# Up to 64 leftover tokens of the first expert moved behind the shared tile; the third expert's loads moved behind the gathers

## The chip, the cores and the metric

One core of one Trainium2 chip runs the program. The metric is device time in microseconds; lower is better. The kernel before took 619.59 us, the median of three runs (619.25 to 619.83).

## The reference

Three layers follow each other on 2304 tokens of 512 numbers: block-causal attention, a dense layer with the maximum of three products, and a routed layer with eight experts. The change is in the last one:

```python
do_compute = x @ w_skip > 0
xc = x[do_compute]
logits = xc @ w_gate
e_idx = np.argmax(logits, axis=1)
gate_w = softmax(logits)[chosen expert]
for e in range(E):
    h = np.maximum(xc[e_idx == e] @ w1[e], 0.0)      # 512 -> 1024
    y[e_idx == e] = gate_w * (h @ w2[e])             # 1024 -> 512
out = x.copy(); out[do_compute] = xc + y
```

For the inputs that are drawn, 532 tokens are computed. By the reference the experts get, sorted by size, 153, 117, 116, 69, 60 and 17 tokens, and two experts get none.

## The kernel before

Attention and the dense layer fill the first 527 us. They write x to DRAM (`x2`) and a table of token numbers by expert. `count` (line 890) ranks the experts by their tokens, writes the ranks to `order` and three numbers to `counts`: `first` (tokens of the largest expert), `kind` and `over`. Class `Moe2` does the routed layer.

An expert has four weight pieces of 1 MB (1,048,576 bytes): `w1` by columns (pieces 0 and 1) and `w2` by rows (2 and 3). Piece i of the expert of rank s is numbered q = 4s + i. A piece is loaded by SP into one of six raw buffers (`raw_of`, line 1055: `raw0` to `raw2`, the first four rows of `xa`, `raw4`, the first four of `xb`) or, for q 22 and 23, into `raw22` and `xgw`. ACT copies the piece to fp32r (`split_hi`, "hi") and DVE writes the rest (`split_lo`, "lo"), in two halves each. The next piece for the same buffer can be loaded only then.

The tokens of an expert are gathered from `x2` by indirect DMAs of POOL, 128 rows of 2 KB each (`gather`). `block(s)` works off the first 128 tokens of the expert of rank s: TensorE does each product in three fp32r passes (hi by hi, lo by hi, hi by lo), 12 matmuls of 512 columns for each half of `w1` and 24 for `w2`. It turns the activations between them (`turn`, four 128x128 transposes) and turns the tokens of the next block. `finish` multiplies by the gate, adds x and scatters the rows to `out`. While block s runs, it splits the pieces q = 4s + 2 to 4s + 5 and orders the loads of q = 4s + 8 to 4s + 11, each behind the splits that free its buffer.

The order of the work is written out by hand in `run`: the gathers, `block(0)`, the gather of the shared tile, `extra`, blocks 1 to 3, `joint`. `extra` works off the tokens 129 to 256 of the largest expert (gathered into `xg2`) by the same 48 matmuls, if `first > P`; `turn_extra` (line 1257, within block 0) turns them. `joint` works off the experts of ranks 4 and 5 in one tile where the second has at most 64 tokens: 64 tokens of each, in native fp32, straight from the raw buffers. `pairs` issues for every contraction slice d two matmuls, one for each expert, that take 64 columns of the array each; TensorE runs a native fp32 matmul as two instructions. So the program waits in `joint` for the raw pieces themselves: q 16 (`raw0`) and q 20 (`raw4`) first.

SP takes its instructions in order: the table loads (`load_table`), the stores of the last x, the loads of q 8 to 11, 22 and 23 (`load_late`), and then those of the blocks. So does POOL: the gathers, then the scatter of each block, and the gather of the shared tile behind the scatter of block 0.

Of the kernel before, what the change touches and what calls it, by code (L numbers as in the profile page):

```python
# [395 lines left out]
@with_exitstack  # L396
def kernel(
    ctx: ExitStack,
    tc: tile.TileContext,
    kqT: bass.AP,  # L400
    kq0: bass.AP,
    v: bass.AP,
    w1: bass.AP,
    w2: bass.AP,
    w3: bass.AP,
    w_out: bass.AP,
    w_route: bass.AP,
    m2_w1: bass.AP,
    m2_w2: bass.AP,
    cst: bass.AP,  # L410
    aux: bass.AP,
    out: bass.AP,
):
# [24 lines left out]
    row0 = const.tile([P, 1], F32, name="row0")  # L438
    two = const.tile([P, 2], F32, name="two")
    wr_sb = const.tile([P, ND, NG], F32, name="wr_sb")  # L440

    _moe1_phase(tc, nc, const, small, locals())


def _moe1_phase(tc, nc, const, small, g):
# [12 lines left out]
    with ExitStack() as st_y:  # L458
# [431 lines left out]
        def count():  # L890
# [7 lines left out]
            first, kind, over = (by[:, n:n + 1] for n in range(3))  # L898
# [3 lines left out]
            nc.vector.tensor_copy(first, by[:, 3:4])  # L902
# [5 lines left out]
            nc.vector.tensor_tensor(two[:, 0:1], used[:, 1:2], used[:, 2:3], op=ALU.is_gt)  # L908
            nc.vector.tensor_copy(counts, by[0:1])
# [17 lines left out]
        def constants():  # L927
# [4 lines left out]
            nc.gpsimd.memset(ones, 1.0)  # L932
            nc.gpsimd.iota(tid, pattern=[[P, NT // P]], base=0, channel_multiplier=1,
# [95 lines left out]
class Moe2:  # L1029
    def __init__(self, tc, nc, small, ypool, tmp, wpool, xp, ps_m, g):  # L1030
# [3 lines left out]
        self.order, self.pick, self.two = g["order"], g["pick"], g["two"]  # L1034
# [6 lines left out]
        self.xg4 = self.right.tile([P, DM], F32, name="xg4")  # L1041
        self.lo = []
# [21 lines left out]
    def load(self, e, i, raw):  # L1064
# [5 lines left out]
        self.nc.sync.dma_start(out=raw, in_=src.rearrange("o (c p) n -> p (o c) n", p=P))  # L1070

    def load_q(self, q, raw=None):
        self.load(self.eid[q // 4], q % 4, self.raw_of(q) if raw is None else raw)
# [40 lines left out]
    def load_table(self):  # L1114
        small, sync, table = self.small, self.nc.sync, self.table
        self.te = small.tile([P, NE, 2], F32, tag="te", name="te", bufs=1)
        self.te1 = small.tile([P, 2], F32, tag="te1", name="te1", bufs=1)
        self.te5 = small.tile([P, NE, 2], F32, tag="te5", name="te5", bufs=1)
        tv = table.rearrange("(e n) t -> n e t", e=NE)
        sync.dma_start(out=self.te, in_=tv[0:P])  # L1120
        sync.dma_start(out=self.te1, in_=table[bass.ds(self.eid[0] * CAP + P, P), :])
        sync.dma_start(out=self.te5[64:P], in_=tv[0:64])

    def load_late(self):
        self.get_order(range(2, 6))
        self.load_raws(12)
        self.raw22 = self.ypool.tile([P, 4, 512], F32, tag="h_h", name="raw22")
        for i in (2, 3):
            self.load_q(20 + i, self.joint_w(1, i))
# [73 lines left out]
    def block(self, s, load=True, nxt=True, plain=False):  # L1203
# [52 lines left out]
        if s == 0:  # L1256
            self.turn_extra()
# [83 lines left out]
    def index_tables(self):  # L1341
# [11 lines left out]
        nc.vector.tensor_copy(tt[:, NE, :], self.te1)  # L1353
# [4 lines left out]
    def index_joint(self):  # L1358
# [11 lines left out]
        nc.vector.tensor_copy(ti[r, 4:5], tt[r, 4, 0:1])  # L1370

    def run(self):
# [3 lines left out]
        first, kind, over = self.regs  # L1376
# [15 lines left out]
        with tc.If(kind > 2, preferred_fallthrough_block=False) as branch:  # L1392
# [99 lines left out]
```

## Time and profile before

| | |
|---|---|
| median of three runs | 619.59 us (619.25 to 619.83) |
| the profiled execution | 618.85 us |
| its span, first to last instruction | 616.9 us |
| PE busy | 595.0 us (96%) |
| DVE, ACT, POOL busy | 57%, 51%, 7% |
| mean granted TensorE clock | 0.997 |
| moved by DMA | 68.65 MB, mean 111 GB/s |

The span is what the instruction records cover; 1.95 us of the execution's time lie around it. A busy PE is not PE at its peak, since matmuls are pipelined; PEld is the loading of weights, which runs beside them, and the start of a weight load shows best when TensorE goes on. The granted clock 1.0 is 2.4 GHz and 0.5 is 1.2 GHz. In the timeline, a bracket tells how long the engine was idle before and what released it.

### The profile page before, as it was taken

The numbers are of one execution on the slowest core, as the hardware profiler recorded it, in microseconds if no ns is written. First come the engines' busy times: TensorE is split into PE (matmuls) and PEld (weight loads), VectorE is DVE, ScalarE is ACT, GpSimd is POOL, SyncE is SP. The second block draws the span as 40 slices with busy tenths as digits, with TensorE's granted clock in tenths as the row PEclk, the third lists the DMA queues.
The fourth block names the chain that finished last, engine by engine and source line by source line (L and its number), as shares of the span: only waits on it lengthen the run. The fifth ranks groups of instructions, "written<-read, shape, count | busy, mean of one in ns | idle before, by whom it ended". The sixth has DMA issues, their size and how long they took to land. (4 is left out here: it accounts for less than half of the span.)

```text
span 616.9 us, 11455 instructions
## 1 busy us (share of the span) xinstructions
PE 595.0 (96%) x4164; PEld 494.2 (80%) x4164; DVE 350.2 (57%) x1001; ACT 316.2 (51%) x816; POOL 44.1 (7%) x99
## 2 busy tenths in 40 slices
PE   6889999999999999999999999999999999999995
PEld 3568797779888888987888887988888997778851
DVE  4899999833645426655165563465642675317920
ACT  4998769933656424545145444446541541236820
POOL 1000000002000010000100001000002002311100
PEclk9999999999999999999999999999999999999998
DMA  6565654321101120102211222200005841695960
GB/s 184 154 202 161 190 158 153 118 90 55 54 28 41 54 88 24 40 24 68 92 44 51 60 75 89 61 22 23 1 25 189 301 153 50 195 380 191 313 231 19
DMA packets 58887, 68.65 MB, mean 111 GB/s; under 512 B 7380, under 2 KB 40404, under 8 KB 58816
## 3 DMA queue, kind: packets, MB, share of 16 engines
q1 hardware_dynamic: 57152, 64.68, 33.0%
q0 software_dynamic: 1664, 3.09, 1.5%
q8 instruction: 37, 0.61, 0.4%
q14 instruction: 34, 0.28, 0.2%
HBM read 57.06 MB, written 11.18 MB: 111 GB/s over the span
## 5 line engine op out<-in xcount | busy, mean ns | idle before, releaser
L730 PE MATMUL ps_h<-x,w 128*128 128x384 f32 x1296 | 243.3, 341 | 0.0
L730 PEld LDWEIGHTS ps_h<-x,w 128*128 128x128 f32 x1296 | 222.8, 188 | 5.9 <-issue 4.7
L650 ACT ACTIVATE p<-sc,nm 128x288 f32<-128x288 f32 (+7 forms) x168 | 84.8, 515 | 27.4 <-DVE nm L639 26.7
L690 ACT COPY pT<-tp 128x512 f32<-128x512 f32 (+2 forms) x106 | 52.2, 505 | 56.3 <-PE tp L685 55.3
L605 PE MATMUL sc<-k,q 64*64 64x288 f32 (+9 forms) x384 | 67.8, 454 | 6.6 <-DMA q<-in_kq_dram 5.0
L685 PE MATMUL tp<-cst_sb,p 128*128 128x128 f32 x432 | 65.8, 281 | 3.9 <-ACT pT L690 1.8
L625 DVE TENSOR_REDUCE nm<-sc 128x2 f32<-128x256 f32 (+7 forms) x64 | 51.5, 812 | 21.3 <-PE sc L612 16.7
L685 PEld LDWEIGHTS tp<-cst_sb,p 128*128 128x128 f32 x432 | 50.0, 142 | 16.7 <-issue 6.9
L704 PE MATMUL pv<-pT,vt 128*64 128x128 f32 (+1 forms) x960 | 60.4, 270 | 1.6 <-ACT pT L690 1.5
L704 PEld LDWEIGHTS pv<-pT,vt 128*64 128x64 f32 x960 | 48.0, 138 | 15.0 <-issue 7.3
L605 PEld LDWEIGHTS sc<-k,q 64*128 64x128 f32 (+1 forms) x384 | 29.6, 179 | 24.1 <-issue 11.1
L671 ACT ACTIVATE p<-p,r 128x512 f32<-128x512 f32 (+8 forms) x74 | 42.9, 597 | 8.8 <-DVE r L665 8.1
L739 DVE TENSOR_TENSOR hm<-ps_h,ha 128x384 f32<-128x384 f32 x36 | 20.0, 556 | 48.1 <-PE ps_h L730 48.0
L771 PE MATMUL ps_y<-wo_h,h_h 128*128 128x512 f32 x108 | 43.8, 405 | 0.0
L771 PE MATMUL ps_y<-wo_l,h_h 128*128 128x512 f32 x108 | 42.3, 392 | 0.0
L771 PE MATMUL ps_y<-wo_h,h_l 128*128 128x512 f32 x108 | 42.2, 391 | 0.0
L776 ACT COPY y<-ps_y 128x512 f32<-128x512 f32 x17 | 9.9, 585 | 53.6 <-PE ps_y L771 46.6
L739 DVE TENSOR_TENSOR hm<-ps_h,hm 128x384 f32<-128x384 f32 x36 | 20.0, 556 | 28.9 <-PE ps_h L730 28.4
L714 ACT CAST x<-pv 128x128 fp32r<-128x128 f32 (+1 forms) x80 | 20.1, 259 | 29.9 <-PE pv L704 29.4
L650 ACT ACTIVATION_READ_ACCUMULATOR p<-sc,nm 128x1 f32 x168 | 34.9, 208 | 0.0
L647 POOL MEMSET p<- 128x128 f32 (+1 forms) x48 | 9.2, 196 | 338.6 <-PE tp L685 214.1
L712 DVE TENSOR_TENSOR x<-pv,x 128x128 fp32r<-128x128 f32 (+1 forms) x80 | 21.2, 275 | 21.1 <-ACT x L714 20.1
(204 smaller groups left out, 755.6 us busy)
## 6 DMA issues: line engine op xcount, KB each, us to landing
raw<-in_m_w_dram SPq DMA_DIRECT2D x16, 1024.0 KB, 7.4
raw<-in_w_dram SPq DMA_DIRECT2D x18, 512.0 KB, 4.2
vt<-in_v_dram SPq DMA_DIRECT2D x16, 320.0 KB, 3.2
x<-y SPq DMA_DIRECT2D x18, 256.0 KB, 2.1
out_dram<-y SPq DMA_DIRECT2D x18, 256.0 KB, 2.4
xa<-in_m_w_dram SPq DMA_DIRECT2D x4, 1024.0 KB, 6.4
raw<-in_w_out_dram SPq DMA_DIRECT2D x6, 512.0 KB, 3.5
xb<-in_m_w_dram SPq DMA_DIRECT2D x3, 1024.0 KB, 8.3
```

What stands on the lines that cost most here:

```text
L605: nc.tensor.matmul(bank[:, 0:hi - lo], gd["q"][rows, q0:q0 + nq], gd["k"][rows, lo:hi], start=True, stop=packed or hi != nk)
L625: nc.vector.tensor_reduce(nm, first_ps[:, :, 0:w], axis=AX.X, op=ALU.max, negate=True)
L650: nc.scalar.activation(u["p"][:, j, lo:hi], src, AF.Exp, bias=u["nm"][:, j:j + 1], scale=0.125, accum_out=u["su"][:, n, j:j + 1])
L671: nc.scalar.activation(pt, pt, AF.Copy, scale=r)
L685: nc.tensor.transpose(tp[:, n, :], u["p"][:, j, t * P:(t + 1) * P], ident)
L690: copy(u["pT"][:, m:m + z], u["tp", m][:, 0:z])
L704: nc.tensor.matmul(pv[64 * j:64 * j + 64, 0:nq], vt[:, t, 64 * j:64 * j + 64], pT, start=(t == 0), stop=(t == nkt - 1))
L712: nc.vector.tensor_tensor(xl, pv, xh, op=ALU.subtract)
L714: nc.scalar.copy(xh, pv)
L730: nc.tensor.matmul(ps, a[:, d, :], x[:, d, :], start=(n == 0), stop=(n == 3 * ND - 1))
L739: nc.vector.tensor_tensor(nxt, hm_at["ps", i], hm_at[f], op=ALU.max)
L771: nc.tensor.matmul(ps, a[:, f, hs], x[:, f, :], start=(n == 0), stop=(n == 3 * NF - 1))
```

## The change

- `count` computes two numbers more. `few` is 1 if the largest expert has 129 to 192 tokens and the ranks 4 and 5 share a tile; `more` is 1 if it has over 128 tokens and `few` is 0. `extra` runs if `more > 0`, and `turn_extra` stands there and no longer in block 0.
- With `few`, `joint(True)` does the leftover tokens, up to 64, as well. It loads the four pieces of the first expert again, into the buffers that the joint tile has used up (`raw0`, `raw4`, `raw1`, `raw5` = `xb`). `few_first` multiplies by `w1`, one half of its 1024 columns in each 64 columns of the array; `few_second` multiplies by `w2`, with 256 of 512 output columns in each. A token is thus two rows of 256 numbers, gathered into `xe2` by indices 2t and 2t + 1 and scattered in the same way. `half` holds 0 for the first 64 partitions and 1 for the others.
- `te5` and two copies of the leftover's table rows are loaded behind the stores of x instead of ahead of them.
- The gathers go in the order of ranks 1, 0, 2, leftover, 3, with `xe2` behind them. The loads of q 8, 9, 10, 11, 22 and 23 stand in `load_third`, and the first of them waits for the gather of rank 3 to have landed.

The core of the diff:

```diff
--- before.py
+++ after.py
@@ count @@
-            first, kind, over = (by[:, n:n + 1] for n in range(3))
+            more, kind, over, first = (by[:, n:n + 1] for n in range(4))
+            few = small.tile([P, 1], F32, tag="few", name="few", bufs=1)
...
-            nc.vector.tensor_copy(first, by[:, 3:4])
+            nc.vector.tensor_scalar(more, first, float(P), None, op0=ALU.is_gt)
...
+            nc.vector.scalar_tensor_tensor(few, first, float(P + 64), more, op0=ALU.is_le, op1=ALU.mult)
+            nc.vector.tensor_tensor(kind, kind, used[:, 2:3], op=ALU.add)
+            nc.vector.tensor_tensor(few, few, two[:, 0:1], op=ALU.mult)
+            nc.vector.tensor_tensor(more, more, few, op=ALU.subtract)
+            nc.vector.tensor_tensor(kind, kind, few, op=ALU.add)
@@ Moe2.__init__ @@
+        self.xe2 = self.right.tile([P, 256], F32, name="xe2")
@@ load_table, load_late @@
-        self.te1 = small.tile([P, 2], F32, tag="te1", name="te1", bufs=1)
-        self.te5 = small.tile([P, NE, 2], F32, tag="te5", name="te5", bufs=1)
+        self.te1 = small.tile([P, 2, 2], F32, tag="te1", name="te1", bufs=1)
...
-        sync.dma_start(out=self.te5[64:P], in_=tv[0:64])
 
     def load_late(self):
+        sync = self.nc.sync
+        self.te5 = self.small.tile([P, NE, 2], F32, tag="te5", name="te5", bufs=1)
+        sync.dma_start(out=self.te5[64:P], in_=self.table.rearrange("(e n) t -> n e t", e=NE)[0:64])
+        for j in range(2):
+            sync.dma_start(out=self.te1[64 * j:64 * j + 64, 1], in_=self.table[bass.ds(self.eid[0] * CAP + P, 64), :])
         self.get_order(range(2, 6))
-        self.load_raws(12)
+
+    def load_third(self, after):
+
         self.raw22 = self.ypool.tile([P, 4, 512], F32, tag="h_h", name="raw22")
-        for i in (2, 3):
-            self.load_q(20 + i, self.joint_w(1, i))
+        for q in (8, 9, 10, 11, 22, 23):
+            load = self.load_q(q, self.joint_w(1, q - 20) if q > 12 else None)
+            if q == 8:
+                self.tc.add_manual_dep(load.ins, after.ins.name, mybir.DependencyInfo(
+                    mybir.DependencyClass.Sync, mybir.DependencyReason.DATA), reason="the rows go first")
@@ block @@
-        if s == 0:
-            self.turn_extra()
         self.mm(psy, 4, q + 3, 0, 12, 12, 24)
@@ joint and its helpers @@
-    def joint(self):
-
-        psa, pst, psy = self.psa, self.pst, self.psy[0]
+    def halves(self, t):
+        return t.rearrange("n (h d) -> (n h) d", h=2)
+
+    def few_load(self, lo):
+        self.fw = [self.raw[i] for i in (0, 4, 1, 5)]
+        for i in (lo, lo + 1):
+            self.load(self.eid[0], i, self.fw[i])
+
+    def few_turn(self):
+        ps, x = self.psb[1][:, 0:2 * P], self.xo[:, 2, 256:512]
+        for t in range(2):
+            self.nc.tensor.transpose(ps[:, t * P:(t + 1) * P], self.xe2[:, t * P:(t + 1) * P], self.ident)
+        self.nc.scalar.copy(x, ps)
+
+    def few_first(self):
+        x = self.xo[:, 2, 256:512]
+        for d in range(4):
+            for j in range(2):
+                self.nc.tensor.matmul(self.psb[0][64 * j:64 * j + 64], x[:, d % 2 * P + d // 2 * 64:][:, 0:64],
+                                      self.fw[j][:, d, :], start=(d == 0), stop=(d == 3))
+
+    def few_second(self):
+        h = self.xg2.rearrange("p (c t) -> p c t", c=4)
+        for f in range(8):
+            for j in range(2):
+                self.nc.tensor.matmul(self.psb[1][64 * j:64 * j + 64, 0:256], h[:, f % 4, f // 4 * 64:][:, 0:64],
+                                      self.fw[2 + f // 4][:, f % 4, 256 * j:256 * j + 256], start=(f == 0), stop=(f == 7))
+
+    def joint(self, few):
+
+        nc, psa, pst, psy = self.nc, self.psa, self.pst, self.psy[0]
         self.pairs(psa[0], 0, 0, 0, 4, 0, 4)
+        if few:
+            self.few_load(0)
         self.relu(0, psa[0])
         self.pairs(psa[1], 0, 1, 0, 2, 0, 4)
         self.turn(self.h[0], pst[0])
         self.plain(1, pst[0])
+        if few:
+            self.few_turn()
         self.pairs(psa[1], 0, 1, 2, 4, 0, 4)
+        if few:
+            self.few_load(2)
...
-        self.pairs(psy, 2, 3, 0, 4, 4, 8)
+        if few:
+            self.few_first()
+            self.relu(0, self.psb[0])
+            self.pairs(psy, 2, 3, 0, 2, 4, 8)
+            self.turn(self.h[0], pst[0])
+            nc.scalar.copy(self.xg2, pst[0])
+            self.pairs(psy, 2, 3, 2, 4, 4, 8)
+        else:
+            self.pairs(psy, 2, 3, 0, 4, 4, 8)
         self.finish(psy, self.xg(4), self.ti[:, 4:5], self.tt[:, 4, 1:2], self.xo[:, 0])
+        if few:
+            self.few_second()
+            o = self.xo[:, 2, 0:256]
+            nc.vector.scalar_tensor_tensor(o, self.psb[1][:, 0:256], self.te1[:, 1, 1:2], self.xe2, op0=ALU.mult, op1=ALU.add)
+            nc.gpsimd.indirect_dma_start(
+                out=self.halves(self.out[:, :]), out_offset=bass.IndirectOffsetOnAxis(ap=self.t2s, axis=0),
+                in_=o, in_offset=None, bounds_check=2 * NT - 1, oob_is_err=False)
@@ index_joint @@
+        nc.vector.tensor_scalar(t2, self.te1[:, 1, 0:1], 2.0, self.half, op0=ALU.mult, op1=ALU.add)
+        nc.vector.tensor_scalar(self.t2g, t2, float(2 * NT - 1), None, op0=ALU.min)
+        nc.vector.tensor_copy(self.t2s, t2)
@@ run @@
-        for s, x in ((1, self.xg(1)), (NE, xg2), (0, self.xg(0)), (2, self.xg(2)), (3, self.xg(3))):
-            self.gather(tg[:, s:s + 1], x)
+        for s, x in ((1, self.xg(1)), (0, self.xg(0)), (2, self.xg(2)), (NE, xg2), (3, self.xg(3))):
+            last = self.gather(tg[:, s:s + 1], x)
+        tc.nc.gpsimd.indirect_dma_start(
+            out=self.xe2, out_offset=None, in_=self.halves(self.x2[:, :]),
+            in_offset=bass.IndirectOffsetOnAxis(ap=self.t2g, axis=0))
+        self.load_third(last)
         self.block(0)
         self.gather(tg[:, 4:5], self.xg(4))
-        with tc.If(first > P):
+        with tc.If(more > 0):
+            self.turn_extra()
             psy = self.extra()
```

**SP, from the table loads to block 1.** `raw4` to `raw1` take q 8 to 11, `raw22` and `xgw` q 22 and 23. Before:

```order
L1121 DMA te1_6381<-table_64 128x2 [waits DMAHW0_49]
L1122 DMA te5_6382<-table_64 64x8x2 [waits DMAHW1_49]
L780 DMA x2_63<-y_6390 128x512 [waits DMAHW2_49,DVE_49]
L781 DMA out_0_dram<-y_6390 128x512 [waits DMAHW3_49]
L1070 DMA raw4_6146<-in_m2_w1_dram 128x4x512 [waits DMAHW4_49,PE_49]
L1070 DMA xb_6170<-in_m2_w1_dram 128x4x512 [waits DMAHW5_49]
L1070 DMA raw0_5779<-in_m2_w2_dram 128x4x512 [waits DMAHW6_49]
L1070 DMA raw1_5780<-in_m2_w2_dram 128x4x512 [waits DMAHW7_49]
L1070 DMA raw22_6439<-in_m2_w2_dram 128x4x512 [waits DMAHW0_49,PE_49]
L1070 DMA xgw_6171<-in_m2_w2_dram 128x4x512 [waits DMAHW1_49,Pool_49]
```

Now:

```order
L1130 DMA te1_6391<-table_64 128x2 [waits DMAHW0_49]
L781 DMA x2_63<-y_6398 128x512 [waits DMAHW1_49,DVE_49]
L782 DMA out_0_dram<-y_6398 128x512 [waits DMAHW2_49]
L1135 DMA te5_6403<-table_64 64x8x2 [waits DMAHW3_49]
L1137 DMA te1_6391<-table_64 64x2 [waits DMAHW4_49]
L1137 DMA te1_6391<-table_64 64x2 [waits DMAHW5_49]
L1080 DMA raw4_6150<-in_m2_w1_dram 128x4x512 [waits DMAHW6_49,DMASW0_49,PE_49]
L1080 DMA xb_6174<-in_m2_w1_dram 128x4x512 [waits DMAHW7_49]
L1080 DMA raw0_5782<-in_m2_w2_dram 128x4x512 [waits DMAHW0_49]
L1080 DMA raw1_5783<-in_m2_w2_dram 128x4x512 [waits DMAHW1_49]
L1080 DMA raw22_6491<-in_m2_w2_dram 128x4x512 [waits DMAHW2_49,PE_49]
L1080 DMA xgw_6175<-in_m2_w2_dram 128x4x512 [waits DMAHW3_49,Pool_49]
```

The loads of `te5` and of two halves of `te1` have moved behind the stores, and the load into `raw4`, ahead of all the others, has one wait more, for DMASW0, which is the semaphore of the fifth gather.

**POOL, the gathers up to the branch at `extra`.** `xa` and `xb` take the rows of ranks 0 to 3, `xo` those of the leftover (`xg2`), `xg4` those of the shared tile. Before:

```order
L1159 DMA xa_5835<-x2_63,tg_6446 128x512 [waits DMAHW3_49,DMAHW2_49,DMAHW5_49,DVE_49,Pool_49]
L1159 DMA xo_6442<-x2_63,tg_6446 128x512 [waits DMASW5_49,PE_49]
L1159 DMA xa_5835<-x2_63,tg_6446 128x512 [waits DMASW6_49,DMASW0_49]
L1159 DMA xb_6170<-x2_63,tg_6446 128x512 [waits Pool_49] x2
L1337 DMA out_0_dram<-xo_6442,ti_6445 2304x512 [waits DMAHW4_49,DMAHW3_49,DMAHW6_49,DMASW1_49,DVE_49]
L1159 DMA xg4_5787<-x2_63,tg_6446 128x512 [waits DMASW2_49,Pool_49]
L1387 COMPARE_AND_BRANCH
```

Now:

```order
L1177 DMA xa_5839<-x2_63,tg_6451 128x512 [waits DMAHW3_49,DMAHW1_49,DMAHW5_49,DVE_49,Pool_49]
L1177 DMA xa_5839<-x2_63,tg_6451 128x512 [waits DMASW5_49,DMASW0_49,PE_49]
L1177 DMA xb_6174<-x2_63,tg_6451 128x512 [waits DMASW6_49,Pool_49]
L1177 DMA xo_6447<-x2_63,tg_6451 128x512 [waits PE_49]
L1177 DMA xb_6174<-x2_63,tg_6451 128x512 [waits Pool_49]
L1455 DMA xe2_5791<-x2_63,t2g_6480 128x256 [waits DMASW1_49,DVE_49]
L1402 DMA out_0_dram<-xo_6447,ti_6450 2304x512 [waits DMAHW4_49,DMAHW2_49,DMAHW6_49,DMASW2_49,DVE_49]
L1177 DMA xg4_5790<-x2_63,tg_6451 128x512 [waits DMASW3_49,Pool_49]
L1461 COMPARE_AND_BRANCH
```

The leftover's gather has moved from the second place to the fourth, and a sixth gather, of `xe2`, stands ahead of block 0's scatter and of the shared tile's gather.

## Rows read from the trace of the kernel before

**Rows 1.** PE weight loads (PEld) from block 0's end to block 1's start: start us, us.

```profile
537.65 0.88 PEld L1200 LDWEIGHTS psy<-hi,Two_l 128*128 128x128 f32 x4
540.72 0.42 PEld L1166 LDWEIGHTS psb<-cst_sb,xo 128*128 128x128 f32 x4 [2.18 <-DMA xo<-x,tg]
541.11 0.78 PEld L1200 LDWEIGHTS psy<-hi,Two_h 128*128 128x128 f32 x4
...
543.77 0.87 PEld L1200 LDWEIGHTS psb<-hi,Two_h 128*128 128x128 f32 x4
...
554.72 0.87 PEld L1200 LDWEIGHTS psy<-hi,Two_l 128*128 128x128 f32 x4
555.63 0.41 PEld L1200 LDWEIGHTS psa<-hi,Two_h 128*128 128x128 f32 x2
```

**Rows 2.** Timeline of the shared tile and the end, all engines.

```profile
592.79 0.19 PEld L1279 LDWEIGHTS psa<-raw,xa 128*64 128x64 f32 x2 [0.35 <-issue]
...
594.02 0.20 PEld L1279 LDWEIGHTS psa<-raw,xa 128*64 128x64 f32 x4 [1.05 <-SPq L1392]
...
599.32 0.42 PEld L1166 LDWEIGHTS pst<-cst_sb,h 128*128 128x128 f32 x4 [0.81 <-issue]
...
599.90 0.13 PEld L1279 LDWEIGHTS psa<-raw,xa 128*64 128x64 f32 x1 [0.17 <-issue]
...
605.42 0.14 PEld L1279 LDWEIGHTS psy<-xa,xb 128*64 128x64 f32 x1 [0.29 <-issue]
...
608.86 0.59 PE L1279 MATMUL psy<-xgw,xb 128*64 128x512 f32 x1
609.58 0.75 DVE L1336 SCALAR_TENSOR_TENSOR xo<-psy,tt,xg 128x512 f32<-128x512 f32 x1 [15.93 <-PE psy L1279]
```

**Rows 3.** Timeline of SP: the last store, the third expert's first load, q 20's load.

```profile
528.62 0.43 SPq L781 DMA_DIRECT2D out_dram<-y  x1
532.13 0.39 SPq L1070 DMA_DIRECT2D raw<-in_m_w_dram  x1
...
585.92 0.37 SPq L1070 DMA_DIRECT2D raw<-in_m_w_dram  x1
```

**Rows 4.** DMA issues, 585 to 587 us: KB each, us to landing.

```profile
raw<-in_m_w_dram SPq DMA_DIRECT2D x1, 1024.0 KB, 8.1
```

**Rows 5.** DMA issues, 558.5 to 560 us (nothing else loading).

```profile
raw<-in_m_w_dram SPq DMA_DIRECT2D x1, 1024.0 KB, 5.1
out_dram<-xo,ti POOLq DMA_INDIRECT x1, 3.0
```

**Rows 6.** Three stretches: busy of PE, PEld, DVE, ACT, POOL, PEclk, DMA share, GB/s.

```profile
541.00:555.00 14.00, 14.00 (x69) 11.58 (x68) 2.83 (x4) 4.85 (x7) 1.98 (x2) 1.00 1.03 383
573.00:588.00 15.00, 15.00 (x75) 12.42 (x74) 14.33 (x16) 12.23 (x16) 1.71 (x1) 1.00 0.95 309
588.00:595.00 7.00, 6.83 (x33) 4.36 (x33) 2.21 (x3) 1.07 (x2) 0.97 (x1) 1.00 1.04 391
```

**Rows 7.** Timeline of POOL: the first and the fifth of five gathers.

```profile
531.16 0.99 POOL L1159 DMA_INDIRECT xa<-x,tg  x1 [10.34 <-DVE tt L1368]
...
536.23 0.94 POOL L1159 DMA_INDIRECT xb<-x,tg  x1 [0.30 <-issue]
```

**Rows 8.** DMA issues, 531 to 532.3 us: the first gather.

```profile
xa<-x,tg POOLq DMA_INDIRECT x1, 3.7
```

**Rows 9.** Timeline: block 1's copy of the third expert's weights, block 2's first weights.

```profile
562.54 1.04 ACT L1152 CAST hi<-raw 128x1024 fp32r<-128x1024 f32 x1
...
567.89 0.19 PEld L1200 LDWEIGHTS psa<-hi,Two_h 128*128 128x128 f32 x1
```

**Rows 10.** Timeline of DVE: its next work behind the index instructions.

```profile
534.58 0.69 DVE L1185 TENSOR_TENSOR Two_l<-pst,Two_h 128x512 fp32r<-128x512 f32 x1 [3.19 <-ACT Two_h L1181]
```

**Rows 11.** Stretches behind the last matmul: the granted clock (PEclk) before the DMA share.

```profile
612.50:613.00 0.50, 0.00 (x0) 0.00 (x0) 0.00 (x0) 0.00 (x0) 0.00 (x0) 1.00 0.24 66
...
613.50:614.00 0.50, 0.00 (x0) 0.00 (x0) 0.00 (x0) 0.00 (x0) 0.00 (x0) 0.50 0.06 25
```

More of the change, by code (lines that the diff above doesn't have):

```diff
@@ L439 @@
     two = const.tile([P, 2], F32, name="two")
+    half = const.tile([P, 1], F32, name="half")
     wr_sb = const.tile([P, ND, NG], F32, name="wr_sb")
@@ L932, in constants @@
             nc.gpsimd.memset(ones, 1.0)
+            for j in range(2):
+                nc.gpsimd.memset(g["half"][64 * j:64 * j + 64], float(j))
             nc.gpsimd.iota(tid, pattern=[[P, NT // P]], base=0, channel_multiplier=1,
@@ L1033, in __init__ @@
         self.x2, self.table, self.out, self.counts, self.ident = (g[n] for n in ("x2", "table", "out", "counts", "ident"))
-        self.order, self.pick, self.two = g["order"], g["pick"], g["two"]
+        self.order, self.pick, self.two, self.half = (g[n] for n in ("order", "pick", "two", "half"))
         self.m2_w1, self.m2_w2 = g["m2_w1"], g["m2_w2"]
@@ L1069, in load @@
             src = self.m2_w2[e, (i - 2) * 512:(i - 1) * 512, :]
-        self.nc.sync.dma_start(out=raw, in_=src.rearrange("o (c p) n -> p (o c) n", p=P))
+        return self.nc.sync.dma_start(out=raw, in_=src.rearrange("o (c p) n -> p (o c) n", p=P))
     def load_q(self, q, raw=None):
-        self.load(self.eid[q // 4], q % 4, self.raw_of(q) if raw is None else raw)
+        return self.load(self.eid[q // 4], q % 4, self.raw_of(q) if raw is None else raw)
     def load_raws(self, limit):
@@ L1280, in pairs @@
                                       start=(n0 + d == 0), stop=(n0 + d == n1 - 1))
-    def joint(self):
-        psa, pst, psy = self.psa, self.pst, self.psy[0]
+    def halves(self, t):
[18 more added lines that the diff above has]
+        for f in range(8):
+            for j in range(2):
+                self.nc.tensor.matmul(self.psb[1][64 * j:64 * j + 64, 0:256], h[:, f % 4, f // 4 * 64:][:, 0:64],
+                                      self.fw[2 + f // 4][:, f % 4, 256 * j:256 * j + 256], start=(f == 0), stop=(f == 7))
+    def joint(self, few):
+        nc, psa, pst, psy = self.nc, self.psa, self.pst, self.psy[0]
         self.pairs(psa[0], 0, 0, 0, 4, 0, 4)
+        if few:
+            self.few_load(0)
         self.relu(0, psa[0])
@@ L1352, in index_tables @@
             self.pick.unsqueeze(2).to_broadcast([P, NE, 2, NE]), op=ALU.mult)
-        nc.vector.tensor_copy(tt[:, NE, :], self.te1)
+        nc.vector.tensor_copy(tt[:, NE, :], self.te1[:, 0])
         nc.vector.tensor_reduce(tt[:, 0:NE], tb, axis=AX.X, op=ALU.add)
@@ L1370, in index_joint @@
         nc.vector.tensor_copy(ti[r, 4:5], tt[r, 4, 0:1])
+        t2 = small.tile([P, 1], F32, tag="t2h", name="t2h", bufs=1)
+        self.t2g, self.t2s = (small.tile([P, 1], I32, tag=n, name=n, bufs=1) for n in ("t2g", "t2s"))
+        nc.vector.tensor_scalar(t2, self.te1[:, 1, 0:1], 2.0, self.half, op0=ALU.mult, op1=ALU.add)
+        nc.vector.tensor_scalar(self.t2g, t2, float(2 * NT - 1), None, op0=ALU.min)
+        nc.vector.tensor_copy(self.t2s, t2)
     def run(self):
@@ L1375, in run @@
         xg2 = self.xg2
-        first, kind, over = self.regs
+        more, kind, over = self.regs
         self.h = [self.tmp.tile([P, 512], F32, tag="y", name=f"h{i}") for i in range(2)]
@@ L1391, in run @@
             self.block(s, plain=s == 3)
-        with tc.If(kind > 2, preferred_fallthrough_block=False) as branch:
+        with tc.If(kind > 3, preferred_fallthrough_block=False) as branch:
             self.get_order(range(6, NE))
@@ L1400, in run @@
                 self.block(s, load=s < 6)
-            with tc.If(kind > 3):
+            with tc.If(kind > 4):
                 self.block(7, load=False, nxt=False)
         with branch.Else():
-            with tc.If(kind > 1) as branch:
-                self.joint()
-            with branch.Else():
+            with tc.If(kind < 2, preferred_fallthrough_block=False) as branch:
                 with tc.If(kind > 0):
@@ L1409, in run @@
                     self.block(4, load=False, nxt=False)
+            with branch.Else():
+                with tc.If(kind > 2) as branch:
+                    self.joint(True)
+                with branch.Else():
+                    self.joint(False)
         with tc.If(over > P):
```

2 lines of the change are left out of this document (1 added, 1 removed).

## The prediction

> **What bounds the kernel now.** TensorE is busy for 96% of the span, so I read the last 90 us as a chain of TensorE's weight loads, and at each gap ask what ended it. The timeline of block 0's end [rows 1] shows one gap: a group of four weight loads starts at 537.65, the turn of the leftover tokens waits until 540.72 for their gather, and the next group starts at 541.11. The same rows show `extra` from 543.77 to 555.63 without a gap, and what a group of four takes: 554.72 to 555.63, 0.91 us. The timeline of the shared tile [rows 2] shows a second gap. Its first pair starts at 592.79, and the pair's second half goes on only at 594.02. That row names SP; the DMA issues tell what it was: piece q 20 (`raw4`) is issued at 585.92 and lands 8.1 us later [rows 3, 4], at 594.02. A piece that is alone lands 5.1 us after its issue [rows 5]. So the loads already run late at the end of the kernel before, and what comes after 594.02 is a chain of TensorE alone.
>
> The view that decides here is that of the stretches [rows 6]: with several pieces queued the DMA engines move 383 GB/s (541 to 555, a gather and a scatter among the pieces) and 391 GB/s (588 to 595), but 309 GB/s from 573 to 588.
>
> **What is taken off TensorE's path.** `extra` goes: 555.63 - 543.77 = 11.86 us [rows 1]. The turn of the leftover and its wait go: 541.11 - 537.65 - 0.91 = 2.55 us. Together 14.4 us: by TensorE alone, the shared tile could start at 592.79 - 14.4 = 578.4. The copies of `turn_extra` on ACT and DVE, and the branch around `extra`, lie beside other work; a bubble at the branch is at most of the size of the 0.35 us ahead of the shared tile [rows 2], and the loads (below) cover it.
>
> **What is added to TensorE's path, in the shared tile.** (a) Two transposes: the four of a `turn` take from 599.32 to 599.90, 0.58 [rows 2]; two, 0.3. (b) `few_first`: four slices of two matmuls side by side, as in `pairs`. The second half of the tile's `w2`, 605.42 to 608.86, is eight steps of 0.43 (the last begins at 608.86), two to a slice [rows 2]: 8 x 0.43 = 3.4. (c) One more turn: 0.58 and 0.1 around it, 0.7. (d) `few_second`: eight slices, 16 steps, of 256 columns. If a step halves with its columns, 16 x 0.215 = 3.4; if it can't get shorter, 16 x 0.43 = 6.9. I take 3.4, since 0.43 is just two passes of 512 columns at 2.4 GHz, so that the columns set it. With 0.1 for its start: 7.9 us.
>
> **The tail.** The last DVE instruction has half the columns: 0.75 us [rows 2] falls to about 0.4. But the last scatter waits for the tile's own scatter, which starts some 1.2 us after the tile's last matmul (0.75 of it that instruction) and lands 3.0 us later [rows 5]; (d) hides all but a few tenths of that. Between -0.4 and +0.3; I take -0.2.
>
> **What the moved loads cost.** The fifth gather starts at 536.23 [rows 7]; a first gather landed 3.7 us after its start [rows 8], and a scatter of as many rows in 3.0 [rows 5]. With no pieces beside it I take 3.7: 539.9, against 532.13 for the first load before [rows 3]. Behind that wait on SP stand q 8 to 11, 22, 23 and then everything that blocks 1 to 3 order. The first piece lands 5.1 later, at 545.0. Until q 20 lands, 14 pieces more must pass (q 9 to 11, 22, 23, 12 to 20): 14 x 1.049 = 14.7 MB, and beside them the scatters of blocks 0 to 2 and the shared tile's gather, 128 rows of 2 KB each (0.26 MB), and `xe2` (0.13): 1.2 MB. From 545.0 on the queue never runs dry: each load is ordered by the blocks some 10 us before its turn. 15.9 MB at 391 GB/s are 40.6 us: **q 20 lands at 585.6**. At 383 it is 586.4; at 400 and with a gather of 3.0 us, 584.2. That is 7 us after TensorE could begin: the loads bound the tile's start, and the 14.4 us become 594.02 - 585.6 = 8.4.
>
> Lateness within the blocks is paid out of the same wait. ACT copies q 8 at 562.54 in block 1; a block is 567.89 - 555.63 = 12.26 us [rows 1, 9]; so it wants q 12 at 562.54 + 12.26 - 14.4 = 560.4, and that lands at 545.0 + 6.9 MB / 391 GB/s = 562.8. Some 2 us late, it moves block 2's end, but not q 20. If the loads were faster, this would be up to 2 us on the path.
>
> The leftover's own pieces (4 MB) have cover: the first two are issued when the first group of pairs ends, 3.4 us after q 20, and land within 0.4 + 7.7 (5.1 [rows 5] and one piece's 2.7 more): at 11.5. `few_first` stands where the tile's last group stood, 605.42 - 594.02 = 11.4 [rows 2], plus (a): 11.7. That is close; 1 us late would be 1 us on the path. The other two have 4 us to spare.
>
> **Edits at nothing.** The six DVE instructions in `count` fill idle DVE time while TensorE multiplies. On SP three loads now come behind the store that is issued at 528.62 [rows 3]; at 0.43 to 0.5 for an issue, as that store's, and at most 3.0 to land, as the scatter [rows 5], `te1` is there at 533.5; DVE's next work behind the index instructions starts at 534.58 [rows 10], and the three new ones end by 534. With this cover gone each us late would hold block 0. POOL reaches `xe2` only after five gathers at 537.5.
>
> **Sum.** -8.4 + 7.9 - 0.2 = -0.7 us, set against the profiled execution, 618.85 to 618.15. The median of the three runs lies 0.74 above that execution, so I forecast **618.9** for the median. Differences below 0.2% (1.24 us) count as no change, about what a measurement of this kernel can tell apart: 618.35 to 620.83. The bounds of the loads alone give 617.5 to 619.7.
>
> **Rivals.**
> - *The loads run slower than 391 GB/s* (slower, 622). For it: 309 GB/s from 573 to 588 [rows 6], where DVE and ACT split pieces all the time, as they do in the stretch that now decides. Against it: the loads were then also ordered late, one or two at a time, so engines ran dry. If only the four pieces of rank 4 go at 309, 4.19 MB take 13.6 instead of 10.7 us: +2.9, 621.8. It decides from about 370 GB/s on (+2.3). The Trainium skill (DMA: Bandwidth & Descriptors, Where 436 GB/s comes from) speaks for it: the HBM side, about 358 GB/s a core, should bind such transfers; worked out from that page, an estimate, 15.9 MB take 44.3 us and the time is 622.6. The trace disagrees as long as it shows 383 to 391 for whole stretches. 18%.
> - *TensorE's clock falls in its new wait* (slower). TensorE ends block 3 near 580 and waits 4 to 6 us for q 20; no gap in blocks 0 to 3 is that long now. Behind the last matmul (608.86 and 0.59) the granted clock is 1.00 until 613.0 and 0.50 from 613.5 [rows 2, 11]; the wait that I expect is about as long as that idle stretch. If the first group of pairs, 3.4 us, runs at 1.2 GHz, it costs 3.4 more: 622.3; half of that if the clock rises midway, 620.6. The Trainium skill (TensorE: Matmul & The Clock Gate, HAM oscillation) tells of the same: waits for DMA in which the clock falls back and the next matmuls start at half rate. No run here shows the clock rise again. 10%.
> - *The loads don't bind* (faster). If q 20 lands by 578.4 or so, -14.4 + 7.9 remain, 613.1. That would need some 475 GB/s from 545.0 on, or loads that don't wait for the gather; part of the way is likelier than all. 12%.
> - *The small matmuls don't shorten, or the leftover's pieces come late*: up to +3.4, 622.3. 6%.
> - *The change isn't reached*: with 153 tokens and 60 and 17 on the shared tile, `few` is 1; only an error in the numbers would leave `extra` in place, 619.6. 2%.
>
> **How the numbers follow.** My forecast has 52%, with its own range 617.1 to 620.1; nearly half of that is below 618.35. Faster: 0.25 of it, 0.12 from the rival of free loads, 0.02 from milder forms of the others, 0.39. No change: 0.26, and 0.06 from the cheap ends of the clock and late-piece cases and the unreached change, 0.32. Slower: the rest, 0.29. The range reaches from 616.0, where free loads go half way, to 623.2, past the slow rivals; beyond lie the full -6.5 and a rate near 309 throughout.
>
> **What would show it.** After: no `extra` and no wait near 540; five gathers that land some 3 to 4 us after their start; `raw4` first issued near 540; DMA at 385 GB/s or more from 543 to 585; then a gap of 4 us or more ahead of the shared tile's second matmul, ended by q 20 near 585.6; 3.4 us each for the two new groups; TensorE's last matmul near 609. I am wrong if the tile starts near 579 without a gap, if the DMA share dips while loads are queued, or if the granted clock shows below 1.00 between 580 and 592.

## The result, and the profile after

The kernel is slower: 625.09 us, the median of 6 runs (623.76 to 626.37), against 619.71 of the kernel before on the same chips; the ratio is 1.0082 (95% interval 1.0061 to 1.0103). The forecast was 618.9, and the time lies above its range, which ended at 623.2. The profiled execution took 624.67 us, its span is 622.8 (616.9 before), and the mean granted clock 0.990 (0.997).

`extra` and the wait for the leftover's gather are gone. The timeline of the changed kernel (start us, us, and in brackets the idle time before and its releaser) shows on SP and on PEld what stands between the table loads and block 1, where [rows 1, 3] showed `extra` and the first load at 532.13:

```profile
529.92 1.22 SPq L1137 DMA_DIRECT2D te<-table  x2
...
540.77 0.40 SPq L1080 DMA_DIRECT2D raw<-in_m_w_dram  x1
```

```profile
540.24 0.76 PEld L1218 LDWEIGHTS psy<-hi,Two_h 128*128 128x128 f32 x4 [1.68 <-ACT Two_h L1199]
...
543.42 0.76 PEld L1218 LDWEIGHTS psa<-hi,Two_h 128*128 128x128 f32 x4 [0.56 <-issue]
```

The first load goes out at 540.77 (forecast 539.9). Block 1 starts at 543.42, not at 555.63 [rows 1]: 12.2 of the forecast 14.4 us are there; what is missing is a wait of 1.68 us behind an ACT copy, and 0.56 at the branch. The timeline of the shared tile and the end, against [rows 2]:

```profile
582.45 1.07 PE L1295 MATMUL psa<-raw,xa 128*64 128x512 f32 x2
...
587.60 6.27 PE L1295 MATMUL psa<-raw,xa 128*64 128x512 f32 x16 [4.08 <-DMA raw<-in_m_w_dram]
...
593.03 5.62 SPq L1080 DMA_DIRECT2D raw<-in_m_w_dram  x3
...
595.51 0.66 PE L1184 MATMUL pst<-cst_sb,h 128*128 128x128 f32 x4
...
602.26 3.60 PE L1316 MATMUL psb<-raw,xo 128*64 128x512 f32 x16
...
610.14 0.75 DVE L1401 SCALAR_TENSOR_TENSOR xo<-psy,tt,xg 128x512 f32<-128x512 f32 x1 [26.83 <-PE psy L1295]
611.16 0.97 POOL L1402 DMA_INDIRECT out_dram<-xo,ti  x1 [26.60 <-DVE xo L1401]
613.62 0.48 DVE L1359 SCALAR_TENSOR_TENSOR xo<-psb,te,xe 128x256 f32<-128x256 f32 x1 [2.73 <-PE psb L1323]
615.85 0.97 POOL L1360 DMA_INDIRECT out_dram<-xo,t2s  x1 [3.71 <-issue]
```

The tile's first pair begins at 582.45 and goes on only when q 20 has landed, at 587.60. Then the first group of pairs is slow, as the weight loads show, which begin 0.85 us apart (0.43 before, eight steps in 3.4 us [rows 2]):

```profile
587.60 0.30 PEld L1295 LDWEIGHTS psa<-raw,xa 128*64 128x64 f32 x4 [4.96 <-DMA raw<-in_m_w_dram]
588.51 0.24 PEld L1295 LDWEIGHTS psa<-raw,xa 128*64 128x64 f32 x2 [0.61 <-issue]
589.36 0.24 PEld L1295 LDWEIGHTS psa<-raw,xa 128*64 128x64 f32 x2 [0.62 <-issue]
```

The stretches of the same kernel say why (us, busy of PE, PEld, DVE, ACT, POOL, then PEclk, DMA share, GB/s):

```profile
531.00:541.00 10.00, 8.75 (x44) 6.96 (x43) 2.90 (x12) 2.86 (x5) 5.75 (x6) 1.00 0.53 148
541.00:555.00 14.00, 13.85 (x66) 11.08 (x66) 10.29 (x11) 9.90 (x13) 1.98 (x2) 1.00 0.95 345
555.00:570.00 15.00, 13.86 (x66) 11.06 (x66) 11.68 (x12) 10.58 (x14) 1.26 (x1) 1.00 1.05 390
570.00:582.00 12.00, 12.00 (x60) 9.83 (x59) 8.88 (x10) 7.02 (x10) 1.72 (x1) 1.00 1.05 390
582.00:588.00 6.00, 1.92 (x7) 0.57 (x7) 0.75 (x1) 0.00 (x0) 0.97 (x1) 0.84 1.05 387
588.00:595.00 7.00, 7.00 (x22) 1.95 (x18) 0.00 (x0) 0.60 (x1) 0.00 (x0) 0.65 0.19 47
```

The granted clock is below 1.00 in the last two. Taken by the microsecond, it falls to 0.50 (1.2 GHz) within the gap and is back at 1.00 (2.4 GHz) at 593:

```profile
585.00:586.00 1.00, 0.00 (x0) 0.00 (x0) 0.00 (x0) 0.00 (x0) 0.00 (x0) 1.00 1.06 387
586.00:587.00 1.00, 0.00 (x0) 0.00 (x0) 0.00 (x0) 0.00 (x0) 0.00 (x0) 0.54 1.03 379
...
592.00:593.00 1.00, 1.00 (x6) 0.37 (x4) 0.00 (x0) 0.00 (x0) 0.00 (x0) 0.54 0.00 0
593.00:594.00 1.00, 1.00 (x6) 0.28 (x4) 0.00 (x0) 0.01 (x1) 0.00 (x0) 1.00 0.00 0
```

From q 20's landing to the tile's first turn it is 595.51 - 587.60 = 7.91 us; it was 599.32 - 594.02 = 5.30 [rows 2].

From these rows the span's growth of 5.9 us adds up:

| stretch | before, us | after, us | difference | forecast |
|---|---|---|---|---|
| span's start to q 20's landing | 594.02 | 587.60 | -6.42 | -8.4 |
| to the tile's first turn | 5.30 | 7.91 | +2.61 | 0 |
| to the tile's last DVE instruction | 10.26 | 14.63 | +4.37 | +4.4 |
| to the leftover's DVE instruction | - | 3.48 | +3.48 | +3.5 |
| to the span's end | 7.32 | 9.18 | +1.86 | -0.2 |

### The profile page after: what moved, and what is told of

Read it like the earlier page. It is cut to its first block, busy times and chain, and to the rows that moved or that the text cites. A ratio compares the mean times of both kernels' runs of the same rounds, so it can differ in the third digit from the quotient of the medians.

```text
span 622.8 us, 11474 instructions
## 1 busy us (share of the span) xinstructions
PE 594.5 (95%) x4158; PEld 488.4 (78%) x4158; DVE 349.1 (56%) x1006; ACT 315.4 (51%) x814; POOL 44.4 (7%) x102
```

## The experiments

The theory after this: q 20 binds the tile, and the change took away the time that covered its loading; in the gap the clock falls (theory L). Rivals: the new groups are the loss (W), contention with the gathers (C). Each run is compared with the kernel before on the same chip; intervals are 95%. Where one run is set against another, their medians can come from different chips, on which the kernel before took 619.51 to 619.71 us.

**The loads without the wait.**

```diff
-            if q == 8:
-                self.tc.add_manual_dep(load.ins, after.ins.name, ...)
```

> The changed kernel with one thing undone: the third expert's six loads no longer wait for the fifth gather. Theory L (the wait for the gathers is what costs: it moves every later piece, TensorE stands ahead of the shared tile until q 20 lands at 587.60, and its clock falls there): the first load goes out near 531, q 20 lands near 580 (594.02 of before less the 14.4 us taken off TensorE), no gap over 1.5 us ahead of the tile's second matmul, granted clock 1.00 until after the last matmul; 7.6 us for the loads and 2.6 for the clock come off 625.1: 615, between 613.5 and 616.5. Rival W (the leftover's new work and the tail are the loss, the loads matter little): 623 to 625. Rival C (the gathers, now among the pieces, land late and hold block 0's end or block 1): 618 to 621, with a wait for a gather of 3 us or more between 537 and 556.

Measured: 622.98 us, ratio 1.0050 (1.0034 to 1.0066). Theory L in this form missed by 8 us. The timeline and the stretches:

```profile
581.28 1.07 PE L1292 MATMUL psa<-raw,xa 128*64 128x512 f32 x2
...
585.68 3.05 PE L1292 MATMUL psa<-raw,xa 128*64 128x512 f32 x8 [3.33 <-DMA raw<-in_m_w_dram]
```

```profile
531.00:541.00 10.00, 8.78 (x43) 6.70 (x42) 2.69 (x11) 2.86 (x5) 5.73 (x6) 1.00 0.75 225
541.00:555.00 14.00, 13.85 (x66) 11.08 (x65) 10.28 (x12) 9.65 (x13) 3.05 (x2) 1.00 1.02 352
```

The first load goes out at 535.37, 5.4 us earlier, yet q 20 lands only 1.9 us earlier. In 531 to 555 just (225 - 148) x 10 + (352 - 345) x 14 = 868 KB more pass than in the changed kernel, 2.2 us of DMA at 390 GB/s. The wait is a small part of the gap; the larger one is that the pieces up to q 20 fill the DMA engines with or without it (389 to 396 GB/s from 548 to 582 in this run, 389 to 390 in the changed kernel). C in the form put down is out: no wait for a gather of 3 us appears. But the pieces do move slowly while these gathers are among them (250 GB/s from 540 to 544); the last section comes back to it.

**TensorE kept busy in the gap.**

```diff
+        for n in range(5):
+            nc.tensor.matmul(self.psb[0], self.ident, self.raw22[:, n % 4, :], start=(n == 0), stop=(n == 4))
         self.pairs(psa[0], 0, 0, 0, 4, 0, 4)
```

> The changed kernel with five more matmuls of 128x512 (native fp32, into a buffer that is overwritten later, nothing of the result) ahead of the shared tile's first group, in the gap in which TensorE waits for q 20. Theory L with the clock: they fill some 4.3 of the 5.0 us, end before q 20 lands at 587.6, and the granted clock stays at 1.00 from 583 on; the first groups of the tile run at 0.43 us a step and not 0.85: 2.6 us off 625.1, 622.5. Rival K (the fall of the clock is not the idle gap's doing, or the matmuls take as long at the half clock because something else holds them): clock 0.5 again, 625. If the five take longer than the gap, the time is above 625.

Measured: 622.47 us, ratio 1.0044 (1.0029 to 1.0058): 2.6 less, as expected. In this execution the blocks lay 1 us later; timeline and stretches:

```profile
583.49 4.45 PE L1330 MATMUL psb<-raw,cst_sb 128*128 128x512 f32 x10
587.88 4.58 PE L1295 MATMUL psa<-raw,xa 128*64 128x512 f32 x18
...
594.10 0.66 PE L1184 MATMUL pst<-cst_sb,h 128*128 128x128 f32 x4
```

```profile
588.80 0.20 PEld L1295 LDWEIGHTS psa<-raw,xa 128*64 128x64 f32 x4 [0.74 <-DMA raw<-in_m_w_dram]
```

```profile
582.00:588.00 6.00, 6.00 (x19) 3.02 (x18) 0.75 (x1) 0.00 (x0) 0.97 (x1) 1.00 1.05 387
588.00:595.00 7.00, 7.00 (x32) 2.42 (x34) 0.00 (x0) 0.76 (x2) 0.00 (x0) 1.00 0.51 185
```

The clock stays at 1.00, and from q 20's landing to the turn it is 594.10 - 588.80 = 5.30 us, exactly as before the change. The fall of the clock is caused by the gap and costs 2.6 us.

**The leftover not worked off.**

```diff
                 with tc.If(kind > 2) as branch:
-                    self.joint(True)
+                    self.joint(False)
```

> The changed kernel in which the up to 64 leftover tokens are not worked off at all (their rows are left as they were, the leftover's own pieces are not loaded): the wait, the gap and the fall of the clock stay, the two transposes, few_first, the turn, few_second and the second scatter go. Theory L: the new work costs what the sum said, 7.9 us, and the tail 1.5 to 2.1 more through the last scatter that waits for the tile's own: 615.1 to 615.7, and the gap until 587.6 with the clock at 0.50 unchanged. Rival W (the new work is dearer than the sum, by its loads or its small matmuls): 611 to 613. Rival (the new work lies beside a wait and is nearly free): above 618.

Measured: 614.76 us, ratio 0.9913 (0.9889 to 0.9937), 10.3 less than with it. The timeline of PEld and DVE:

```profile
587.96 0.30 PEld L1295 LDWEIGHTS psa<-raw,xa 128*64 128x64 f32 x4 [5.06 <-SPq L1467]
...
606.22 0.75 DVE L1401 SCALAR_TENSOR_TENSOR xo<-psy,tt,xg 128x512 f32<-128x512 f32 x1 [22.65 <-PE psy L1295]
```

The gap ends at 587.96 and the clock is 0.61 from 588 to 595. From q 20's landing to the last DVE instruction it is 18.26 us, against 613.62 - 587.60 = 26.02 with the leftover: its work is worth 7.8 us, as summed. The span is 613.8, so the tail behind that instruction is 7.58 us against 9.18. The spans differ by 9.0 us; the rest of the 10.3 is not in these two profiles. The work isn't dearer than summed, which leaves W with the tail alone.

**Two pieces later.** q 22 and 23 are read only by the tile's second layer, and stood ahead of q 12.

```diff
-        for q in (8, 9, 10, 11, 22, 23):
+        for q in (8, 9, 10, 11):
...
+        for q in (22, 23):
+            self.load_q(q, self.joint_w(1, q - 20))
         self.pairs(psa[0], 0, 0, 0, 4, 0, 4)
```

> The changed kernel with the wait for the gathers kept, but q 22 and q 23, which only the shared tile's second layer reads, ordered behind q 21 and not ahead of q 12. Theory L: two pieces (2.7 us each) less stand ahead of q 12 to q 20, so q 20 lands near 582.2 and block 2 no longer waits for q 12; the gap ahead of the tile shrinks from 5.0 to under 2 us, the clock stays at 1.00, and 5.1 and 2.6 us come off: 617.4, between 616 and 618.5. If the tile is then held by q 22, 619 to 621. Rival W: 624 to 625.

Measured: 618.95 us, ratio 0.9993 (0.9979 to 1.0008): 6.1 less. The timeline of PE:

```profile
580.94 1.07 PE L1295 MATMUL psa<-raw,xa 128*64 128x512 f32 x2
582.74 3.65 PE L1295 MATMUL psa<-raw,xa 128*64 128x512 f32 x16 [0.72 <-DMA raw<-in_m_w_dram]
...
596.91 3.22 PE L1316 MATMUL psb<-raw,xo 128*64 128x512 f32 x13 [1.11 <-DMA raw<-in_m_w_dram]
```

q 20 lands at 582.74, 4.9 us earlier, for 2.1 MB less ahead of it; the granted clock is 1.00 from 582 to 595. This confirms that bytes ahead of q 20 set the tile's start. The miss of 0.5 us against the range is the second wait: the leftover's first pieces now queue behind q 22 and 23, and `few_first` waits 1.11 us for them.

**The old path, with the new wait.** One number makes `few` 0.

```diff
-            nc.vector.scalar_tensor_tensor(few, first, float(P + 64), more, op0=ALU.is_le, op1=ALU.mult)
+            nc.vector.scalar_tensor_tensor(few, first, float(P), more, op0=ALU.is_le, op1=ALU.mult)
```

> The changed kernel with one number altered in count, so that few is 0 here and the leftover takes the old path: block 0, then its turn and extra, then blocks 1 to 3, with the new order of the gathers and with the third expert's loads still waiting for the fifth gather. It prices the wait where extra's 11.9 us still stand between block 0 and block 1. Theory L, as the runs so far leave it (the wait and the bytes cost only because extra's time is no longer there to cover them): q 20 lands near 587.6 as in the changed kernel and TensorE reaches the tile near 593, so that its gap of 1.23 us goes; the turn of the leftover, now behind block 0 and not inside it, shows 1.7 us of copies: 619.5 against 619.5 before, between 618.5 and 620.5. Rival (the wait itself costs, wherever extra is): 621.5 and more, with a gap ahead of the tile.

Measured: 623.76 us, ratio 1.0062 (1.0046 to 1.0077): the rival's time, though not by its cause. The timeline of PE, and the DMA queues from 593 to 595 us (packets, MB, share):

```profile
592.55 1.09 PE L1218 MATMUL psy<-hi,Two_l 128*128 128x512 f32 x4
...
597.46 2.55 PE L1295 MATMUL psa<-raw,xa 128*64 128x512 f32 x7 [3.82 <-issue]
```

```profile
q1 hardware_dynamic: 370, 0.75, 98.2%
q8 instruction: 1, 0.02, 3.0%
q14 instruction: 2, 0.02, 1.9%
```

The tile's very first matmul, which needs only q 16, starts 3.82 us late and waits for nothing that the profile shows, while packets of the instruction queues pass among the last pieces. The granted clock is 0.83 from 595 to 605. The code for this case had moved behind the code for the leftover, behind a taken branch. The same branch taken the other way tests it:

```diff
-                with tc.If(kind > 2) as branch:
-                    self.joint(True)
+                with tc.If(kind > 1) as branch:
+                    self.joint(False)
```

> The old path with the loads' wait again (few is 0), with the shared tile's code put where TensorE runs straight into it and not behind a taken branch past the code for the leftover. Theory J (of the 4.1 us that the old path lost, the gap of 4.2 us ahead of the tile that no wait in the profile explains is TensorE without instructions after the jump, and the half clock behind it follows from that gap; the wait for the gathers itself is covered by extra): the gap falls to 1.5 us or less, ended by q 20, clock 1.00 through the tile: 2.7 and 1.7 us off 623.8, 619.4, between 618.5 and 620. Rival (the wait for the gathers costs by itself, through the loads): a gap of 3 us or more again, 622.5 or more.

Measured: 618.86 us, ratio 0.9989 (0.9976 to 1.0002), 4.9 less. The first 18 matmuls of the tile run in one piece:

```profile
592.69 4.51 PE L1295 MATMUL psa<-raw,xa 128*64 128x512 f32 x18
```

So the place of the code cost the old path its gap and its clock; the wait for the gathers costs nothing that shows where `extra` stands in front of block 1. The edit also leaves the code for the leftover out of the program, so the two runs don't tell the jump from the amount of code. That the late start is the loading of instructions fits both runs, but no row names it.

**The last scatter free of the tile's.**

```diff
+            self.tc.declare_no_dep(last.ins, tile.ins, reason="disjoint rows")
```

> The changed kernel with the last scatter free of the tile's own scatter (they write disjoint rows), nothing else. Theory T (the last scatter waits for the tile's scatter to land, some 1.5 us past the end of its own data): the last POOL instruction starts 0.6 to 0.8 us after the last DVE instruction starts, near 614.3 and not 615.85: 1.5 us off 625.1, 623.6. Rival (two scatters at once take longer, or the end is set by what comes after the scatter): 625.

Measured: 623.63 us, ratio 1.0062 (1.0049 to 1.0075). The median is what theory T said; the timeline is not:

```profile
612.92 0.48 DVE L1359 SCALAR_TENSOR_TENSOR xo<-psb,te,xe 128x256 f32<-128x256 f32 x1 [2.73 <-PE psb L1323]
613.68 0.97 POOL L1360 DMA_INDIRECT out_dram<-xo,t2s  x1 [2.24 <-DVE xo L1359]
```

The scatter follows its data by 0.76 us and not by 2.23, but the span ends at 621.8: 8.88 us from the last DVE instruction to the end, against 9.18. Only 0.3 of the 1.47 us arrives; 0.9 more came from the gap in this profile, whose first 16 matmuls took 5.35 us instead of 6.27. This profile also shows that the loads bind: block 1 starts at 541.59, 1.83 us earlier than in the changed kernel, and q 20 still lands at 587.83. The lead is waited out in block 2 (3.56 us at 567.15, against 1.58 at 566.98) and ahead of the tile.

**Towards a better version.** First q 22 at the tile's start and q 23 behind the leftover's first two pieces, with the free scatter:

```diff
+        self.load_q(22, self.raw22)
         self.pairs(psa[0], 0, 0, 0, 4, 0, 4)
         if few:
             self.few_load(0)
+        self.load_q(23, self.xgw)
```

> The kernel with two pieces later (618.95), with q 23 behind the leftover's first two pieces, so that these land 2.7 us earlier and few_first no longer waits 1.1 us for them, and with the last scatter free of the tile's: 1.1 and 1.5 us off: 616.4, between 615.5 and 617. Rival: q 23, now ordered near 586.5 behind four pieces, lands after 599 and holds the tile's last layer by 1 us or more: 617.5 and above.

Measured: 617.20 us, ratio 0.9964 (0.9942 to 0.9985), just above the range; its executions spread from 614.48 to 619.6. In its profile TensorE still waits 1.32 us for q 20, and no wait for a piece is left behind that. Then the same without the wait for the gathers:

```diff
         for q in (8, 9, 10, 11):
-            load = self.load_q(q, self.joint_w(1, q - 20) if q > 12 else None)
-            if q == 8:
-                self.tc.add_manual_dep(load.ins, after.ins.name, ...)
+            self.load_q(q)
```

> The same with the wait for the gathers taken away as well. Theory L: without the wait q 20 came 1.9 us earlier in the run that took it away alone; here the gap of 1.6 us ahead of the tile's second matmul goes: 1.0 to 1.6 us less than with the wait, near 615. Rival C (the gathers among the pieces slow block 0's end or the first pieces by as much): no difference to the version with the wait.

Measured: **613.93 us**, ratio 0.9917 (0.9904 to 0.9930): the best version, 5.7 us below the kernel before, with 3.3 us off where 1.0 to 1.6 were expected. The timeline and the stretches:

```profile
579.26 4.51 PE L1292 MATMUL psa<-raw,xa 128*64 128x512 f32 x18
```

```profile
582.00:588.00 6.00, 6.00 (x31) 2.81 (x29) 0.00 (x0) 1.46 (x3) 0.00 (x0) 1.00 0.92 333
588.00:595.00 7.00, 7.00 (x36) 2.42 (x34) 0.00 (x0) 1.18 (x2) 0.00 (x0) 1.00 1.05 389
```

TensorE starts the tile at 579.26, its weight loads wait 0.42 us for q 20 at 579.88, and the clock stays at 1.00. Between the two profiles q 20 lands 1.88 us earlier, as much as in the run that took the wait away alone (1.92), and a little above the expected 1.0 to 1.6. The other 1.1 us are in the tail, 8.02 us from the last DVE instruction to the end against 9.14, which the edit doesn't touch. Part of the best time may be luck: block 1 starts at 541.63 here and at 543.64 in the run without the wait, for a reason that no run isolates (last section). By an estimate, TensorE would come to the tile near 581.3 with that start, 1.4 us after q 20 has landed here. With the wait for the tile's scatter put back into this version:

```diff
-            self.tc.declare_no_dep(last.ins, tile.ins, reason="disjoint rows")
```

> The best version (613.93) with one thing put back: the last scatter waits for the tile's again. With the scatters free on the changed kernel the median fell by 1.46 us, but in its profile the time from the last DVE instruction's start to the end fell only from 9.18 to 8.88 us, though the last scatter started 1.47 us earlier. Theory T (the end follows the last scatter): 1.5 us more, 615.4. Rival E (the end follows something else, the last instructions of the program and what they load, and the 1.46 us of that run came from the shorter gap of its executions): 0 to 0.5 us more, 613.9 to 614.4.

Measured: 615.01 us, ratio 0.9939 (0.9920 to 0.9957). It lies between T and E, and the intervals of the two versions overlap; the profiles give 8.69 us from the last DVE instruction to the end, against 8.02. Over all profiles with both scatters this tail is 8.69 to 9.63 us with the wait and 8.02 to 9.14 without it. How much the wait costs, between 0 and 1.5 us, stays open.

**Whose gain is it?** The order of the pieces alone, in the kernel before:

```diff
     def load_late(self):
...
-        for i in (2, 3):
-            self.load_q(20 + i, self.joint_w(1, i))
...
     def joint(self):
+        for i in (2, 3):
+            self.load_q(20 + i, self.joint_w(1, i))
```

> The kernel before with only q 22 and q 23 ordered behind q 21: how much of the best version's gain belongs to the order of the pieces alone, without the change. Theory L (with extra in place the pieces are ordered by the blocks, late, and nothing of the early bytes binds q 20): no difference, 619.0 to 620.0, q 20 at 594 as before. Rival (the order of the pieces alone brings it): the gap of 1.2 us ahead of the tile goes, 618.3 or less. If q 22 or q 23 come too late for the second layer: 621 and above.

Measured: 619.95 us, ratio 1.0014 (0.9999 to 1.0029): no gain. And the best version with `extra` instead of the small groups (the two edits of the old path in line):

> The best version with few 0 and the shared tile's code in line, so that the leftover is done by extra again: what the small leftover groups earn where no load binds. From the rows: 14.4 less the 2.5 of the turn that now shows behind block 0 in this version anyway, against 7.9 and 1.9 us for the new groups and the tail: the old path is 4 to 6 us slower, 618 to 620. Rival (most of the best version's gain is the order of the loads, whatever does the leftover): under 616.

Measured: 620.11 us, ratio 1.0017 (1.0003 to 1.0032), 6.2 more than the best version. So neither half gains alone: the order of the loads is worth nothing with `extra` in place, and the small groups lose without the order.

## Why the prediction was wrong

- **What is taken off: right in size, not where it ends.** Block 1 starts 12.2 us earlier. That loads bind the tile's start was the forecast's main step and holds: the gap of 4.96 us is there, ended by q 20, and of 14.4 us only 6.4 arrive. The lateness within the blocks came as forecast too: ACT waits 2.49 us for a piece until 565.40 and block 2 then 1.58 us until 566.98, out of the same wait.
- **q 20 at 585.6: 2.0 us too early.** The fifth gather held the first load 0.9 us longer than 3.7 us of landing would have. The rate was right, 387 to 390 GB/s from 555 to 588. The other 1.1 us are mostly bytes: from 545.87, 5.1 us behind the first load, to 587.60 16.24 MB pass, not 15.9, at 389 GB/s. The sum let only the pieces up to q 20 pass, but q 21, ordered at 578.24, moves beside q 20: SP's loads moved 16.46 MB from 540.77 to 587.60, 0.73 more than the 15 pieces up to q 20 hold. The rival of 309 GB/s is out. The Trainium skill (DMA: Bandwidth & Descriptors, Where 436 GB/s comes from) would have these transfers bound at some 358 GB/s a core; this trace disagrees, with 390. It agrees with another page of the Trainium skill (Perfetto Trace Analysis, Roofline), by which a core that is active alone can pull more than that share.
- **The step that failed most: the clock in the new wait.** The forecast put its price at 1.7 to 3.4 us and its chance at 10%, and left it out of the sum, although it expected just the gap that brings it. It cost 2.6 us (7.91 from q 20's landing to the turn, not 5.30), and the run with busy matmuls shows cause and price. The row to trust was there: [rows 11] had the clock at 0.50 after an idle stretch about as long as the gap that the forecast itself worked out. The Trainium skill (TensorE: Matmul & The Clock Gate, HAM oscillation) tells of waits for DMA behind which the next matmuls start at half rate. Here the trace agrees: a clock of 0.50 and 0.85 us a pair behind the gap of 4.96.
- **The new groups: right.** +4.37 and +3.48 against 4.4 and 3.5; matmuls of 256 columns take half the time of 512 (3.48 us for 16 steps), and the pieces of the leftover came without a wait.
- **The tail: wrong by 2.1 us.** The sum took 3.0 us for the tile's scatter to land and found it hidden. The last scatter started 615.85 - 611.16 = 4.69 us behind it and 2.23 us behind its own data, where the free scatter took 0.76: a wait of 1.47 us that the sum had at nothing. The row was near: in the trace of before the tile's scatter, the last one, took 3.8 us to land, while [rows 5] is a block's. From the last scatter's start to the end it then took 622.8 - 615.85 = 6.95 us, against 616.9 - 610.61 = 6.29 before. But taking the wait away brought only 0.3 us at the end of the profile, so what makes a tail of 9 us instead of 7.3 behind two scatters stays open.
- **The rival "the loads don't bind" was wrong in its condition.** It said that loads which don't wait for the gather would give 613.1, and the run without the wait gave 622.98. It takes the wait away and two pieces moved as well, as the best version does.

With 2.0 for q 20, 2.6 for the clock and 2.1 for the tail, the forecast's -0.7 becomes +6.0; the spans grew by 5.9.

## What to carry to other kernels

Time taken off an engine counts only as far as the loads can follow; count the bytes queued ahead of the piece that is needed first, and those that move beside it, and order by when a piece is read, not by when its buffer is free. If a forecast contains a gap in TensorE like this one, of 4 to 5 us, the clock behind it belongs in the sum: here some six pairs at 0.85 us and not 0.43, 2.6 us. And a median that agrees with a theory is no proof of it: the last scatter's run gave the expected time, mostly from another place in the profile.

## What was not expected of the hardware

- Code behind a taken branch started TensorE 3.8 us late, with no wait in the profile; with it put in line, and the code that stood ahead of it left out, the delay was gone and the kernel 4.9 us faster. A branch that is added for one case can cost another.
- In the changed kernel an ACT copy at block 0's end waited until 539.60, 2.4 us past the turn that it copies, for something that the profile calls remote. It came again at the same place in two runs (busy matmuls, leftover not worked off). In the run without the wait 2.35 us of it stood one ACT instruction earlier, and with two pieces later this copy came as late (539.51). It is absent in the other runs, and in the kernel before; where the small groups run without it, block 1 starts near 541.6 and not 543.4. Its cause was not tried.
- Gathers among the loads can slow the engines: in the run without the wait they moved 250 GB/s from 540 to 544 at a DMA share of 1.02; with hardly a gather about, 390 at a share of 1.05. But the kernel before moved 373 GB/s in the same four microseconds at a share of 1.03, with as much gathered (0.59 MB against 0.52). It has no gather of `xe2`; whether that makes the difference was not tried.
